# A clamped sum in one VectorE instruction, squares taken from it, and engines chosen pair by pair

## The chip, the cores and the metric

The kernel runs on 1 core of one Trainium2 chip. The metric is device microseconds for one execution; lower is better. Times of before are 736.77, 738.27 and 739.52 us, median 738.27 us.

The engines are called by the profile's names: PE is TensorE (matmuls), PEld its weight loads, DVE is VectorE, ACT is ScalarE, POOL is GpSimd, SP is SyncE, which here only issues DMAs. Each takes its instructions in program order.

## What is computed

Memory attention for 8 batches of 8 heads (576 tokens, head dimension 64, 32 memories), followed by a feed-forward block with a squared ReLU over the 4608 tokens:

```python
a = exp(phi - max(phi, axis=2)); a = a / (sum(a, axis=2) + 1e-9)
k_m, v_m = einsum('bhsm,bhsd->bhmd', a, k), einsum('bhsm,bhsd->bhmd', a, v)
scores = (1 / sqrt(64)) * q @ k_m.T
attn = exp(scores - max(scores)); attn = attn / (sum(attn) + 1e-9)
x = (attn @ v_m) as (4608, 512)
h = maximum(x @ w_in, 0)          # 512 -> 2048
out = (h * h) @ w_out             # 2048 -> 512
```

## The kernel before

Matmul operands in fp32r are carried as a high and a low part: ACT copies a value into `hi`, another engine writes `lo = value - hi`, and each product takes three matmuls. `w_in` is first multiplied into each batch's memories (`u`), so the first layer is `u` times the attention weights `a`.

Batches 0 to 2 (the first stage, to about 303 us) run one block of 128 hidden units and 288 tokens at a time. Batches 3 to 7 (the late stage) run in 40 pairs: a pair is two blocks of hidden units times two halves of 288 tokens, and its first layer is formed from 7 products of combined operands instead of 8 (`ffn1_product`, a scheme of Strassen's kind). The combined operands of the weights are made in `late_split`, those of the attention weights in `combine`. The 7 products land in three PSUM banks: two of `h`, which change places from pair to pair, and `z`. Four results of a pair come out of them:

- three by `from_sum`: ACT copies `z` into an SBUF tile `x` (`from_z`), DVE adds the `h` bank to it (line 1022), DVE clamps and squares in one instruction into `g` (line 1025), ACT copies `g` into `g_hi` (line 1026), POOL writes `g_lo` (line 1027), and for the second token half ACT also copies 64 columns aside (line 1029);
- one by `from_h`: ACT clamps the bank into `r` (line 1035), squares `r` into `g_hi` (line 1037), DVE multiplies `r` by `r` (line 1039) and subtracts (line 1040).

The second layer's 24 matmuls of a pair (line 984) are queued and issued between the first layer's products: `slot(k, n)` gives n of them in three parts, and ahead of each part `half(h)` issues whatever the plan has put at that half. A pair has 8 halves, a batch 64. The plan's lists (`late_plan`, `next_plan`, `first_plan`) hold, for each side task, the halves at which its steps are issued; numbers count from the batch's first half. Side tasks prepare the next batch: `late_exp` (softmax over phi, mostly DVE), `task_mem`, `late_attend`, `combine`, `late_u` (the products for `u` on PE into bank `m` and the free `h` bank, then two copies out, line 874), `late_split`, and loads on the SP queue (`late_stream` fetches the weights that `late_u` needs). The table `late_on` says for each named step whether POOL (1) or DVE (0) does it.

Of the kernel before, what the change touches and what calls it, by code (L numbers as in the profile page):

```python
# [7 lines left out]

# [16 lines left out]
def attn_moe_kernel(ctx: ExitStack, tc: tile.TileContext, qT, kv, phi, w_in, w_out, outT):  # L25
# [1330 lines left out]
    first_plan = [
        ((18,), task_q, 1, 0),
        ((-2,), task_kv, 1, 0),
        ((5, 9, 9, 10, 10, 13), task_exp, 1),
        ((16, 16, 16, 20), task_mem, 1),  # L1360
        ((26, 26, 27, 30, 30, 30, 31, 32), late_attend, 1, 0),
        ((37, 37, 39, 39, 40, 40, 42, 43), late_attend, 1, 1),
        ((0,), task_kv, 1, 1),
        ((44, 45, 45, 46, 47, 49), combine, 1),
        ((24,), late_stream, 1, 0),
        ((45, 46), late_u, 1, 0),
        ((33,), task_q, 1, 1),
        ((55,), late_stream, 1, 1),
        ((22, 23, 23, 24, 25, 26, 26, 27, 27, 28, 30, 30, 30), late_exp, 2),
        ((57, 57, 58, 59, 60), late_split, 1, 1),  # L1370
        ((21,), task_phi, 2),
        ((20,), task_kv, 2, 0),
# [231 lines left out]
```

## Time and profile before

| | before |
|---|---|
| median of three runs | 738.27 us |
| the profiled execution: time | 737.53 us |
| its span, first to last instruction | 735.7 us |
| busy in the span: PE, PEld | 704.5 us (96%), 588.6 us (80%) |
| DVE, ACT, POOL | 504.6 us (69%), 402.9 us (55%), 337.3 us (46%) |
| mean granted TensorE clock | 0.986 |

The profiled execution's time is 1.8 us more than its span: what lies ahead of the first instruction and behind the last. Its row counts a PE that has matmuls in flight as busy. The granted clock is a share of full speed, 2.4 GHz; half of that, 1.2 GHz, is its lower level.

### The profile page before, as it was taken

What the parts mean: (1) busy time and instruction counts of PE and PEld (TensorE: products, weight loads), DVE (VectorE), ACT (ScalarE), POOL (GpSimd) and SP (SyncE); (2) the same over time, 40 slices, a digit from 0 to 9 for tenths busy, and PEclk for the clock granted to TensorE, in tenths of its full rate; (3) what the DMA queues carried; (4) which work ended last, traced back from release to release, by engine and by line L of the source; (5) the groups of instructions that cost most, each with busy time, mean ns of one, the idle gap of its engine ahead of it and who ended that gap; (6) DMA issues with size and microseconds to landing.
All of it is one profiled execution on the core that took longest, in us unless ns stands there. A gap on an engine that the chain in (4) does not pass through costs nothing.

```text
span 735.7 us, 14219 instructions
## 1 busy us (share of the span) xinstructions
PE 704.5 (96%) x5242; PEld 588.6 (80%) x5242; DVE 504.6 (69%) x1070; ACT 402.9 (55%) x1042; POOL 337.3 (46%) x461
## 2 busy tenths in 40 slices
PE   7899999999999999999889998999899998999997
PEld 4367899899999899887668776787677877878897
DVE  4977757743545666578986788878887888565432
ACT  2657888865444256555445455655545555555431
POOL 1213255452432346465555455664655566555400
PEclk9999999999999999999999999999999999999999
DMA  9994453333076701282116511392112211310011
GB/s 309 346 352 189 141 154 127 109 99 147 33 179 194 201 33 58 98 246 90 58 57 190 156 58 58 114 253 93 58 48 102 90 57 58 115 58 1 0 58 37
DMA packets 65126, 88.81 MB, mean 121 GB/s; under 512 B 6432, under 2 KB 53856, under 8 KB 61600
## 3 DMA queue, kind: packets, MB, share of 16 engines
q1 hardware_dynamic: 63040, 86.33, 36.4%
q10 hardware_dynamic: 2016, 1.57, 0.7%
q8 instruction: 41, 0.67, 0.4%
q14 instruction: 29, 0.24, 0.1%
HBM read 74.25 MB, written 13.63 MB: 119 GB/s over the span
## 4 chain that ended last, share of the span: by engine, by line
PE 72%; DVE 17%; DMA 4%; ACT 4%; issue 2%; POOL 1%; SPq 0%; ACTq 0%; DVEq 0%; POOLq 0%
PE acc L984 20%; PE acc L669 16%; PE h L640 10%; PE h L1008 6%; PE z L1008 5%; PE acc L661 4%; DVE g_lo L1025 2%; PE h L1559 2%; PE ps_m L411 2%; PE m L411 2%; DMA wp<-in_w_in 2%; DMA e_sb<-in_phi 1%; DVE g_hi L1022 1%; DMA u_lo<-in_kv 1%; DVE low L906 1%
## 5 line engine op out<-in xcount | busy, mean ns | idle before, releaser
L984 PE MATMUL acc<-u_hi,wp 128*128 128x512 f32 x480 | 134.9, 401 | 0.0
L653 POOL TENSOR_TENSOR g_lo<-g,g_hi 128x288 fp32r<-128x288 f32 x80 | 71.2, 891 | 121.5 <-ACT g_hi L651 50.9
L984 PE MATMUL acc<-u_lo,wp 128*128 128x512 f32 x480 | 126.3, 400 | 0.0
L984 PEld LDWEIGHTS acc<-u_hi,wp 128*128 128x128 f32 x480 | 87.1, 189 | 34.8 <-issue 19.6
L895 POOL TENSOR_TENSOR u_lo<-low,u_hi 128x256 fp32r<-128x256 f32 (+1 forms) x133 | 89.9, 685 | 44.7 <-ACT u_hi L894 44.2
L984 PEld LDWEIGHTS acc<-u_lo,wp 128*128 128x128 f32 x480 | 90.8, 194 | 16.3
L669 PE MATMUL acc<-g_hi,wp 128*128 128x288 f32 x616 | 99.7, 298 | 0.0
L1027 POOL TENSOR_TENSOR u_hi<-g_lo,u_hi 128x288 fp32r<-128x288 f32 (+1 forms) x78 | 60.4, 775 | 72.8 <-ACT u_hi L1026 61.5
L669 PEld LDWEIGHTS acc<-g_hi,wp 128*128 128x128 f32 x616 | 87.7, 190 | 6.2 <-issue 2.8
L642 ACT ACTIVATE r<-h 128x288 f32<-128x288 f32 x96 | 39.3, 409 | 81.1 <-PE h L640 80.8
L894 ACT CAST u_hi<-low 128x256 fp32r<-128x256 f32 (+1 forms) x133 | 44.3, 351 | 42.5 <-DVE low L906 29.1
L669 PE MATMUL acc<-g_lo,wp 128*128 128x288 f32 x308 | 58.2, 297 | 0.0
L1026 ACT CAST u_hi<-g_lo 128x288 fp32r<-128x288 f32 (+1 forms) x78 | 31.6, 405 | 44.9 <-DVE g_lo L1025 43.8
L1022 DVE TENSOR_TENSOR g_hi<-h,g_hi 128x288 f32<-128x288 f32 x79 | 35.7, 451 | 18.4 <-ACT g_hi L1045 17.9
L669 PEld LDWEIGHTS acc<-g_lo,wp 128*128 128x128 f32 x308 | 47.1, 190 | 0.0
L1027 POOL TENSOR_TENSOR u_lo<-g_lo,u_lo 128x224 fp32r<-128x224 f32 x40 | 27.5, 688 | 41.8 <-ACT u_lo L1026 37.4
L1039 DVE TENSOR_TENSOR g_lo<-g 128x288 f32<-128x288 f32 x40 | 25.9, 648 | 28.4 <-ACT g L1035 28.3
L640 PE MATMUL h<-a_hi,u_hi 128*128 128x288 f32 x192 | 44.4, 317 | 0.6 <-DVE st L760 0.6
L1045 ACT COPY g_hi<-z 128x288 f32<-128x288 f32 x79 | 31.1, 393 | 25.5 <-PE z L1008 25.2
L648 DVE TENSOR_TENSOR g<-h,r 128x288 f32<-128x288 f32 x41 | 18.6, 453 | 35.5 <-ACT r L642 35.2
L1025 DVE SCALAR_TENSOR_TENSOR g_lo<-g_hi 128x288 f32<-128x288 f32 x78 | 41.0, 525 | 2.5
L640 PE MATMUL h<-a_hi,u_lo 128*128 128x288 f32 x176 | 37.5, 294 | 0.0
(335 smaller groups left out, 1677.6 us busy)
## 6 DMA issues: line engine op xcount, KB each, us to landing
w_sb<-w_f SPq DMA_DIRECT2D x23, 1024.0 KB, 4.9
wp<-in_w_in SPq DMA_DIRECT2D x16, 512.0 KB, 8.2
wp<-in_w_out SPq DMA_DIRECT2D x16, 512.0 KB, 6.8
q_sb<-in_q SPq DMA_DIRECT2D x28, 288.0 KB, 4.0
kvb<-in_kv SPq DMA_DIRECT2D x28, 256.0 KB, 5.8
tmp<-in_kv SPq DMA_DIRECT2D x24, 256.0 KB, 5.9
w_f<-w_sb SPq DMA_DIRECT2D x4, 1024.0 KB, 5.0
e_sb<-in_phi SPq DMA_DIRECT2D x7, 512.0 KB, 5.7
```

Of the source, the lines that this page charges most:

```text
L640: nc.tensor.matmul(h[:, :T], u[:, qd, fs], x[:, qd], start=(i == 0), stop=(i == len(todo) - 1))
L642: nc.scalar.activation(r, h[:, :T], AF.Relu)
L653: nc.gpsimd.tensor_tensor(out=g_lo, in0=g, in1=g_hi.bitcast(F32), op=ALU.subtract)
L669: nc.tensor.matmul(acc[e][:, :T], wo[f][:, w, e * P:(e + 1) * P], x, start=first and x is g_hi and w == 0, stop=last and x is g_lo,)
L894: nc.scalar.copy(hi[:, k], x)
L895: by(name).tensor_tensor(out=lo[:, k], in0=x, in1=hi[:, k].bitcast(F32), op=ALU.subtract)
L984: nc.tensor.matmul(late_accs[e], wo[f][:, w, e * P:(e + 1) * P], x, start=f == 0 and first, stop=f == NFT - 1 and last,)
L1008: nc.tensor.matmul(out[:, :T], u[:, lhs], a, start=first and not n, stop=n == 2, skip_group_check=not first)
L1022: nc.vector.tensor_tensor(out=x, in0=u[:, :T], in1=x, op=ALU.add)
L1025: nc.vector.scalar_tensor_tensor(out=g, in0=x, scalar=0.0, in1=x, op0=ALU.max, op1=ALU.mult)
L1026: nc.scalar.copy(g_hi, g[:, :n])
L1027: by(f"c{2 * fi + t}").tensor_tensor(out=g_lo, in0=g[:, :n], in1=g_hi.bitcast(F32), op=ALU.subtract)
```

## The change

`from_sum` forms the clamped sum with one custom DVE instruction (add, then clamp below at 0) into `x`; `g_hi` is then squared from `x` by ACT, and `g` is either a DVE product `x*x` or a second ACT square. `from_h` multiplies the PSUM bank by `r` instead of `r` by `r`, and its clamp may be done by DVE. The copy out of `z` may be done by DVE. `late_on` turns into a bit mask over the eight pairs of a batch, so that each of these choices, and those of `late_split` and `late_u`, differs by pair. Outside the pairs `sub1` and `at1` go to DVE, `mul1` and `b1` to POOL. The plan's halves are new, and `slot` gives 8, 11, 5 second-layer matmuls instead of 7, 11, 6.

```diff
     late_on = {
-        "top": 0, "sub0": 0, "sub1": 1, "sub2": 1, "at0": 0, "at1": 1, "mul0": 0, "mul1": 0,
-        "t3": 0, "t1": 0, "t2": 0, "t4": 0, "b0": 1, "b1": 0, "b2": 0, "b3": 1,
-        "b4": 0, "s1": 0, "s2": 0, "s3": 0, "s4": 0, "l0": 1, "l1": 1, "l2": 1,
-        "l3": 1, "c0": 1, "c1": 1, "c2": 0, "c3": 1, "raw0": 1, "raw1": 1,
+        "m0": 33, "m1": 253, "m3": 160, "fh": 5, "z1": 64, "z2": 4, "z3": 153, "top": 0,
+        "sub0": 0, "sub1": 0, "sub2": 1, "at0": 0, "at1": 0, "mul0": 0, "mul1": 1, "t3": 0,
+        "t1": 0, "t2": 0, "t4": 0, "b0": 1, "b1": 1, "b2": 0, "b3": 1, "b4": 0,
+        "s1": 53, "s2": 207, "s3": 58, "s4": 191, "l0": 187, "l1": 223, "l2": 223, "l3": 185,
+        "c0": 255, "c1": 253, "c2": 6, "c3": 239, "raw0": 14, "raw1": 15,
     }
-    def by(name):
-        return nc.gpsimd if late_on[name] else nc.vector
+    def by(name, p=0):
+        return nc.gpsimd if late_on[name] >> p & 1 else nc.vector
...
     def from_sum(j, fi, t, u, x, name="g_lo", bufs=3):
         g_hi, g_lo, n, kept = squared(j, fi, t)
-        nc.vector.tensor_tensor(out=x, in0=u[:, :T], in1=x, op=ALU.add)
+        nc.vector._custom_dve(TENSOR_ADD_SAT, out=x, in0=u[:, :T], in1=x, s0=float("inf"), s1=0.0)
         yield
         g = work.tile([P, T], F32, name=name, bufs=bufs)
-        nc.vector.scalar_tensor_tensor(out=g, in0=x, scalar=0.0, in1=x, op0=ALU.max, op1=ALU.mult)
-        nc.scalar.copy(g_hi, g[:, :n])
-        by(f"c{2 * fi + t}").tensor_tensor(out=g_lo, in0=g[:, :n], in1=g_hi.bitcast(F32), op=ALU.subtract)
+        nc.scalar.square(g_hi, x[:, :n])
+        if late_on[f"m{k}"] >> p & 1:
+            nc.scalar.square(g[:, :n], x[:, :n])
+        else:
+            nc.vector.tensor_tensor(out=g[:, :n], in0=x[:, :n], in1=x[:, :n], op=ALU.mult)
+        by(f"c{k}", p).tensor_tensor(out=g_lo, in0=g[:, :n], in1=g_hi.bitcast(F32), op=ALU.subtract)
         if kept is not None:
-            nc.scalar.copy(kept, g[:, n:])
+            nc.scalar.square(kept, x[:, n:])
     def from_h(j, fi, t, u):
-        nc.scalar.activation(r, u[:, :T], AF.Relu)
+        if late_on["fh"] >> p & 1:
+            nc.vector.tensor_scalar_max(r, u[:, :T], 0.0)
+        else:
+            nc.scalar.activation(r, u[:, :T], AF.Relu)
         yield
         nc.scalar.activation(g_hi, r[:, :n], AF.Square)
-        nc.vector.tensor_tensor(out=g[:, :n], in0=r[:, :n], in1=r[:, :n], op=ALU.mult)
-        by("c2").tensor_tensor(out=g_lo, in0=g[:, :n], in1=g_hi.bitcast(F32), op=ALU.subtract)
+        nc.vector.tensor_tensor(out=g[:, :n], in0=u[:, :n], in1=r[:, :n], op=ALU.mult)
+        by("c2", p).tensor_tensor(out=g_lo, in0=g[:, :n], in1=g_hi.bitcast(F32), op=ALU.subtract)
-    def from_z(name, bufs):
+    def from_z(j, k, name, bufs):
-        nc.scalar.copy(x, banks["z"][:, :T])
+        (nc.vector.tensor_copy if late_on[f"z{k}"] >> pairs[j][1] & 1 else nc.scalar.copy)(x, banks["z"][:, :T])
...
     late_plan = [
-        ((16, 16), late_u, 0, 2),
+        ((17, 17), late_u, 0, 2),
-        ((21,), late_stream, 0, 3),
+        ((31,), late_stream, 0, 3),
-        ((43, 43, 44, 45, 46), late_split, 0, 7),
+        ((39, 39, 41, 41, 43), late_split, 0, 7),
         ((0, 0), late_u, 0, 1),
         ((32, 32), late_u, 0, 3),
...
     next_plan = [
-        ((49, 49), late_u, 1, 0),
+        ((48, 49), late_u, 1, 0),
-        ((48, 49, 50, 51, 53, 54), combine, 1),
+        ((48, 50, 50, 51, 52, 56), combine, 1),
-        ((40, 40, 41, 41, 43, 44, 45, 46), late_attend, 1, 1),
+        ((40, 41, 41, 41, 44, 45, 46, 48), late_attend, 1, 1),
-        ((25, 25, 26, 26, 26, 29, 32, 32), late_attend, 1, 0),
+        ((25, 25, 25, 26, 26, 27, 32, 34), late_attend, 1, 0),
-        ((49, 49, 50, 55, 55), late_split, 1, 0),
+        ((51, 51, 51, 54, 55), late_split, 1, 0),
-        ((57, 57, 60, 62, 62), late_split, 1, 1),
+        ((57, 59, 59, 63, 63), late_split, 1, 1),
-        ((55, 56, 57, 58, 60, 60, 61, 63, 63, 63, 65, 66, 67), late_exp, 2),
+        ((59, 61, 61, 62, 65, 65, 65, 65, 67, 67, 67, 71, 71), late_exp, 2),
-        ((31,), task_q, 1, 1),
+        ((30,), task_q, 1, 1),
...
     first_plan = [
-        ((26, 26, 27, 30, 30, 30, 31, 32), late_attend, 1, 0),
+        ((29, 29, 29, 33, 33, 33, 35, 35), late_attend, 1, 0),
...
-        counts = {-1: (0, 9, 9), 0: (9, 9, 4)}.get(j, (7, 11, 6))
+        counts = {-1: (0, 9, 9), 0: (9, 9, 4)}.get(j, (8, 11, 5))
```

Lines of the plans are put in pairs here; their order in the file is another. The other entries of the plans move by a few halves as well.

## Rows read from the trace of the kernel before

**Rows 1.** The chain of work that ended last: share of the span by engine.

```profile
PE 72%; DVE 17%; DMA 4%; ACT 4%; issue 2%; POOL 1%; SPq 0%; ACTq 0%; DVEq 0%; POOLq 0%
```

**Rows 2.** Ten stretches, 228 to 728 us: busy us by engine, clock, DMA; their sum.

```profile
228.00:270.00 42.00, 39.68 (x374) 36.27 (x373) 25.54 (x66) 16.93 (x38) 14.22 (x22) 0.96 0.44 127
...
352.00:392.00 40.00, 34.64 (x192) 26.58 (x191) 34.44 (x72) 21.20 (x64) 24.38 (x30) 0.96 0.15 55
...
sum 500.00, PE 481.83 PEld 401.13 DVE 358.11 ACT 257.16 POOL 257.59; mean PE 48.18 PEld 40.11 DVE 35.81 ACT 25.72 POOL 25.76
```

**Rows 3.** The same view, first and last of five stretches with a lower clock.

```profile
248.00:256.00 8.00, 6.33 (x43) 5.18 (x43) 5.65 (x15) 1.57 (x4) 2.85 (x3) 0.79 0.50 133
...
610.00:618.00 8.00, 5.67 (x23) 4.81 (x22) 7.13 (x15) 3.99 (x12) 4.05 (x4) 0.79 0.38 131
```

**Rows 4.** What PE waited for longest: us in total, times, longest.

```profile
PE h L1008 <- ACT low L874: 11.6, 7, 2.3
```

**Rows 5.** Instructions in order of time, 359 to 364.5 us: start, duration, instruction.

```profile
359.40 0.61 PE L411 MATMUL h<-w_sb,mem 64*32 64x512 f32 x1
...
361.93 1.14 DVE L1025 SCALAR_TENSOR_TENSOR g_lo<-g_hi 128x288 f32<-128x288 f32 x1
...
363.54 0.58 ACT L874 COPY low<-h 128x512 f32<-128x512 f32 x1
...
364.17 0.40 PE L1008 MATMUL h<-u_hi,u_hi 128*128 128x288 f32 x1 [2.33 <-ACT low L874]
```

**Rows 6.** DVE groups, 352 to 388 us: count, busy us, mean ns, idle before.

```profile
L1025 DVE SCALAR_TENSOR_TENSOR g_lo<-g_hi 128x288 f32<-128x288 f32 x6 | 3.4, 566 | 0.2
...
L1039 DVE TENSOR_TENSOR g_lo<-g 128x288 f32<-128x288 f32 x3 | 2.3, 779 | 0.0
...
L906 DVE TENSOR_TENSOR low<-low,g_hi 128x128 f32<-128x128 f32 x3 | 1.8, 591 | 0.0
L736 DVE TENSOR_TENSOR e_sb<-e_sb,phi_mx 128x512 f32<-128x512 f32 x1 | 1.8, 1766 | 0.0
...
L724 DVE TENSOR_TENSOR top<-top 32x8 f32<-32x8 f32 x3 | 1.5, 494 | 0.1
L1025 DVE SCALAR_TENSOR_TENSOR g_lo<-g 128x288 f32<-128x288 f32 x3 | 1.4, 451 | 0.1
```

**Rows 7.** Two lines' durations in ns: min/median/max, first and last start.

```profile
L1022 DVE TENSOR_TENSOR g_hi<-h,g_hi x79: 440/451/459, 303.2 to 692.6; 128x288 f32<-128x288 f32 x79
...
L1039 DVE TENSOR_TENSOR g_lo<-g x40: 451/674/1076, 309.8 to 697.5; 128x288 f32<-128x288 f32 x40
```

**Rows 8.** Groups of the whole span, shapes kept apart.

```profile
L984 PE MATMUL acc<-u_hi,wp 128*128 128x512 f32 x480 | 134.9, 401 | 0.0
...
L895 POOL TENSOR_TENSOR u_lo<-low,u_hi 128x128 fp32r<-128x128 f32 x66 | 37.2, 574 | 15.0 <-ACT u_hi L894 14.9
...
L1037 ACT ACTIVATE u_lo<-g 128x288 fp32r<-128x288 f32 x40 | 17.9, 446 | 0.4
...
L562 DVE CUSTOM_DVE_ANT_0 w_sb<-tmp,low 128x2048 uint16<-128x2048 uint16 x4 | 5.3, 1322 | 0.3
```

**Rows 9.** Order of time about the first half of a batch: ACT, PE, DVE.

```profile
380.23 0.41 ACT L1035 ACTIVATE g<-h 128x288 f32<-128x288 f32 x1
...
380.99 0.61 PE L411 MATMUL h<-w_sb,mem 64*32 64x512 f32 x1
...
382.93 0.73 DVE L1039 TENSOR_TENSOR g_lo<-g 128x288 f32<-128x288 f32 x1
```

**Rows 10.** An issue on the SP queue; half 32 on PE and DVE; time to landing.

```profile
331.68 1.85 SPq L400 DMA_DIRECT2D q_sb<-in_q  x2
...
339.55 0.61 PE L411 MATMUL h<-w_sb,mem 64*32 64x512 f32 x1
...
339.95 0.71 DVE L1039 TENSOR_TENSOR g_lo<-g 128x288 f32<-128x288 f32 x1
...
w_sb<-w_f SPq DMA_DIRECT2D x4, 1024.0 KB, 4.9
```

More of the change, by code (lines that the diff above doesn't have):

```diff
@@ L7 @@
 from concourse._compat import with_exitstack
+from concourse.dve_ops import TENSOR_ADD_SAT
 F32 = mybir.dt.float32
@@ L894, in put @@
             nc.scalar.copy(hi[:, k], x)
-            by(name).tensor_tensor(out=lo[:, k], in0=x, in1=hi[:, k].bitcast(F32), op=ALU.subtract)
+            by(name, p).tensor_tensor(out=lo[:, k], in0=x, in1=hi[:, k].bitcast(F32), op=ALU.subtract)
         if b == JOIN and p < 3:
@@ L899, in late_split @@
         s = one.tile([P, 2, P], F32, name="phi_mx") if b == JOIN and p < 3 else work.tile([P, 2, P], F32, name="g_hi", bufs=3)
-        by("s1").tensor_tensor(out=s[:, 0], in0=raw[:, 3], in1=raw[:, 1], op=ALU.add)
-        by("s2").tensor_tensor(out=s[:, 1], in0=s[:, 0], in1=raw[:, 2], op=ALU.subtract)
+        by("s1", p).tensor_tensor(out=s[:, 0], in0=raw[:, 3], in1=raw[:, 1], op=ALU.add)
+        by("s2", p).tensor_tensor(out=s[:, 1], in0=s[:, 0], in1=raw[:, 2], op=ALU.subtract)
         yield
@@ L905, in late_split @@
         put(slice(2, 4), s, "l1")
-        by("s4").tensor_tensor(out=raw[:, 0], in0=raw[:, 0], in1=s[:, 1], op=ALU.subtract)
+        by("s4", p).tensor_tensor(out=raw[:, 0], in0=raw[:, 0], in1=s[:, 1], op=ALU.subtract)
         if b == JOIN and p < 3:
@@ L910, in late_split @@
         put(4, raw[:, 0], "l2")
-        by("s3").tensor_tensor(out=raw[:, 3], in0=raw[:, 2], in1=raw[:, 3], op=ALU.subtract)
+        by("s3", p).tensor_tensor(out=raw[:, 3], in0=raw[:, 2], in1=raw[:, 3], op=ALU.subtract)
         yield
@@ L1326, in attn_moe_kernel @@
     late_plan = [
-        ((10, 10, 10, 13, 14), late_split, 0, 3),
-        ((32, 32), late_u, 0, 3),
-        ((6, 6, 8, 8, 9), late_split, 0, 2),
-        ((0, 0), late_u, 0, 1),
-        ((16, 16), late_u, 0, 2),
-        ((4,), late_stream, 0, 2),
-        ((43, 43, 44, 45, 46), late_split, 0, 7),
-        ((21,), late_stream, 0, 3),
-        ((17, 17, 19, 19, 19), late_split, 0, 4),
-        ((27, 27, 28, 30, 30), late_split, 0, 5),
-        ((34, 35, 35, 35, 36), late_split, 0, 6),
+        ((6, 6, 7, 8, 10), late_split, 0, 2),
@@ L1338, in attn_moe_kernel @@
+        ((17, 17), late_u, 0, 2),
+        ((18, 18, 19, 20, 20), late_split, 0, 4),
+        ((26, 26, 27, 27, 30), late_split, 0, 5),
+        ((10, 10, 10, 11, 13), late_split, 0, 3),
+        ((39, 39, 41, 41, 43), late_split, 0, 7),
+        ((31,), late_stream, 0, 3),
+        ((1,), late_stream, 0, 2),
+        ((0, 0), late_u, 0, 1),
+        ((32, 32), late_u, 0, 3),
+        ((34, 34, 35, 37, 38), late_split, 0, 6),
     ]
     next_plan = [
-        ((36,), late_stream, 1, 0),
-        ((49, 49), late_u, 1, 0),
@@ L1355, in attn_moe_kernel @@
+        ((30,), task_q, 1, 1),
+        ((25, 25, 25, 26, 26, 27, 32, 34), late_attend, 1, 0),
+        ((60,), late_stream, 1, 1),
+        ((23,), task_phi, 2),
+        ((8, 8, 11, 16, 19, 20), task_mem, 1),
+        ((48, 49), late_u, 1, 0),
     ]
     first_plan = [
[L1357 to L1360, printed above, removed]
-        ((26, 26, 27, 30, 30, 30, 31, 32), late_attend, 1, 0),
-        ((37, 37, 39, 39, 40, 40, 42, 43), late_attend, 1, 1),
@@ L1363, in attn_moe_kernel @@
[L1363 to L1372, printed above, removed]
-        ((-5,), task_phi, 1),
-        ((28,), task_kv, 2, 1),
-        ((49, 49, 50, 51, 54), late_split, 1, 0),
+        ((8,), task_q, 1, 0),
@@ new lines, in attn_moe_kernel @@
+        ((43, 44, 44, 47, 47, 47), combine, 1),
+        ((29,), task_kv, 2, 0),
+        ((52, 52, 52, 54, 57), late_split, 1, 0),
+        ((37, 37, 38, 39, 41, 41, 41, 43), late_attend, 1, 1),
+        ((26,), late_stream, 1, 0),
+        ((29, 29, 29, 33, 33, 33, 35, 35), late_attend, 1, 0),
+        ((30,), task_q, 1, 1),
+        ((46,), late_stream, 1, 1),
+        ((22,), task_phi, 2),
+        ((37, 38), late_u, 1, 0),
+        ((-6,), task_phi, 1),
+        ((-13,), task_kv, 1, 1),
+        ((-11,), task_kv, 1, 0),
@@ L1376, in attn_moe_kernel @@
+        ((16, 17, 17, 18), task_mem, 1),
+        ((56, 56, 58, 59, 60), late_split, 1, 1),
+        ((29,), task_kv, 2, 1),
+        ((22, 23, 23, 24, 25, 25, 26, 27, 27, 28, 30, 30, 30), late_exp, 2),
+        ((3, 5, 5, 8, 10, 10), task_exp, 1),
     ]
@@ L1515, in attn_moe_kernel @@
             ffn1_product(z, j + 1, 2, True)
-            x = from_z("g_hi", 3) if old else from_z("r", 2)
+            x = from_z(j + 1, 2, *(("g_hi", 3) if old else ("r", 2)))
         if old:
```

19 lines of the change are left out of this document (10 added, 9 removed).

## The prediction

> **What bounds the kernel now.** I read the chain of waits first: 72% of the span runs through PE, and 17% through DVE, an engine that is busy for only 69% [rows 1]. So DVE is the bound in some stretch. The view by stretches shows where. From 228 to 728 us PE has matmuls in flight for 481.83 of 500 us. The 18.17 us that it lacks lie in five places: 5.36 us are gone between 352 and 392 us, 2.32 us between 228 and 270 us [rows 2], and the other three are the same stretch of the next three batches. In 352 to 392 us DVE is busy for 34.44 of 40 us, POOL for 24.38, ACT for 21.20 [rows 2]. Each of the five places is followed by 8 us in which the granted clock is 0.79, that is, at the lower level for 42% of the time [rows 3]. Half rate for 3.36 us loses 1.68 us; five times, 8.4 us.
>
> So there are 18.2 + 8.4 = 26.6 us to win at most, as long as PE's own work stays. The rest of the late stage is PE from end to end, and no other engine's work there is worth anything.
>
> What PE waits for is the next view: its largest wait is `h` (line 1008) for the ACT copies of line 874, 11.6 us in 7 waits [rows 4]. In order of time one of them reads so: `late_u` writes its results into the `h` bank at 359.40, the bank could be copied out from 360, but ACT takes its instructions in order and stands before a copy of `g` that DVE is late with. DVE starts that `g` at 361.93 and takes 1.14 us; the copy out runs at 363.54, and PE starts at 364.17 after 2.33 us without work [rows 5]. DVE's queue is late, ACT stands behind it, PE stands behind ACT.
>
> **What the change does to that stretch.** The 36 us from 352 to 388 hold three pairs (5 to 7) with one `late_split` each. In DVE time:
>
> - Nine clamp-and-squares of line 1025, six at 566 ns and three at 451 [rows 6], make 4.8 us. Of the nine squares that come in their place the masks leave three on DVE (`m0` of pairs 6 and 7, `m3` of pair 6): 3 x 0.57 = 1.7 us. Less 3.1 us.
> - The three products of line 1039 read two SBUF tiles and take 779 ns each here [rows 6]; over the span 451 to 1076 ns. The addition of line 1022 reads one bank of PSUM, has the same size and takes 440 to 459 ns in all 79 places [rows 7]. The new product reads the bank too: 0.45 us. Less 1.0 us.
> - Of the twelve small operations of `late_split`, four remain on DVE (`s1` and `s3` of pair 7, `s3` of pair 0, `s1` of pair 1). The dearest group, line 906, takes 591 ns [rows 6], the lighter ones less; at about 0.45 us the eight that go are 3.6 us.
> - `b1` goes, a subtract of 288 columns from SBUF, at line 1039's price 0.8 us [rows 6]; `at1` and `mul1`, two operations of one shape, change places: 0.
> - What comes: three copies out of `z` at the 0.45 us of line 1022, one copy of a double bank at ACT's 0.58 us [rows 5], `l3` of pair 1 at about 0.6: 2.5 us.
>
> The custom sum has no row. Below it is bounded by the addition that it replaces, 451 ns [rows 7], above by addition and clamp-and-square one after the other, 451 + 566 ns. The only custom instruction in the trace takes 1322 ns for 1024 words a partition [rows 8], which is 0.37 us for 288 words, so nothing there speaks for a slow one. I take 0.45 us, no change; the upper bound would add 9 x 0.57 = 5.1 us and undo nearly all of the rest.
>
> The sum is -3.1 - 1.0 - 3.6 - 0.8 + 2.5 = -6.0 us. Besides, `late_exp` starts 4 halves later, so that its six small steps (three of them at 494 ns), its subtract of 1.77 us [rows 6] and the two steps between them, some 5 us by estimate, fall into the next batch's first pair. DVE then has 34.4 - 6.0 = 28.4 us, or 23 without the moved part, in a stretch that takes 40 - 5.4 - 1.7 = 33 us when PE doesn't stop: 70 to 86% instead of a queue that is never empty. ACT gains six squares at 446 ns [rows 8] and loses four copies, +1 us. POOL gains eight small operations at 574 ns [rows 8] and `b1`, about +5 us, and passes `l3`: 24.4 + 4.6 = 29 of 33 us, 26 with its part of `late_exp` moved.
>
> The chain of a result gets shorter too: ACT's `g_hi` waits for the sum and no longer for sum and square, one operation of 0.45 to 1.14 us less ahead of the copies of line 874. And `late_u` of pair 6 is issued one half earlier than its copies out, so that eight instead of five second-layer matmuls cover them.
>
> I take three quarters of what the four late stretches lose: idle 18.17 - 2.32 = 15.85 us, clock 6.72 us; 0.75 x 22.6 = 16.9 us. Not all, since the order of each queue is fixed and short waits remain. In the first stage `late_attend` goes three halves behind a burst of `late_exp`; half of 2.32 + 1.68 us, 2.0 us. Together 18.9 us.
>
> **What it costs.** Two new waits on PE's own path.
>
> The `h` bank. Before, ACT's clamp of line 1035 was the last reader of the bank; now the DVE product is. The next user is a side task at the first half of the next pair (halves 0, 32, 40, and now 48). In the trace the clamp starts at 380.23 and ends at 380.64, the side task's matmuls write the bank at 380.99, and the product of line 1039 ran only from 382.93 to 383.66 [rows 9]. With a free DVE the product would end about 0.55 us behind the clamp, against 0.35 us here, and `slot` now gives one matmul less in between (134.9 us for 480, 0.28 us [rows 8]). A wait of some 0.4 us at 16 places (four in each of four batches): 7 us. The ends are 0 (the queue's other work lets PE run late anyway) and the 2.7 us of this place; at half 32 the product would have ended at 340.66, 1.1 us behind the side task's 339.55 [rows 10]. All that is queued on PE waits behind it. I take the low value, because what stood ahead of the product moves: the sum of `late_attend` from half 29 to 27, the small steps of `late_exp` from 60 to 65, `mul1` to POOL.
>
> The weights of `late_u`. `late_stream` for half 32 moves from half 21 to 31 and thereby behind `task_q`, which SP could issue only at 331.68 with 1.85 us for it, since it waits for `late_attend`'s matmuls at half 25; the weights land 4.9 us after their issue, near 338.5, and PE wants them at 339.55 [rows 10]. A margin of 1 us; I put 0.3 us at each of four places, 1.2 us. What stands behind it on SP has time.
>
> The sum against the profiled execution: 737.53 - 18.9 + 7.0 + 1.2 = 726.8 us. The median of the runs lies 0.74 us above that execution, so I predict 727.5 us.
>
> **A rule against it.** POOL's 574 ns for 128 columns [rows 8] stand against DVE's 591 ns for the same shape in the crowded stretch [rows 6]: nothing is lost by the move itself. The Trainium skill, "GPSIMD Engine Reference", 4.1 Engine selection, speaks against it: elementwise work of two inputs belongs on VectorE, GpSimd being about half as fast. By that rule the eight moves would cost POOL about 7 us where DVE saves 3.6, POOL would be at 32 of 33 us, and the sum would come out as rival (a) instead; no row here shows the factor of two.
>
> **The rivals.** Their times are on the scale of the median, 0.7 us above the profiled execution.
>
> (a) POOL takes DVE's place: 29 of 33 us is 88%, in order, behind ACT's copies, and DVE's transposes of `late_attend` now wait for POOL's `mul1`. Against it: the low parts are made about 8 halves, some 10 us, ahead of their use. If POOL is late the stretch stays as long as it is, and only the first stage's 2 us come back: 736 us. The Trainium skill, same page, 1 Specifications, says that GpSimd shares its SBUF interfaces with VectorE, so that each would slow the other; the spread of line 1039 against line 1022 [rows 7] agrees, and what more POOL work does to it no run here shows.
>
> (b) DVE stays the bound, because the custom sum or the squares cost more than I took. With the upper bound of 5.1 us DVE is back at 33 of 33 us, unless the moved `late_exp` gives room; if a quarter comes back instead of three, and the bank's waits fall half into stalls that are there anyway: 738.3 - 5.6 - 2.0 + 3.5 = 734 us.
>
> (c) The other side: the product holds the `h` bank at the 16 places as long as the old queue would have held it. The two places shown would have been late by 1.1 and 2.7 us [rows 9, 10], 1.9 us on average, 30 us in all: 738.3 - 18.9 + 30 + 1.2 = 751 us. It decides from 18.9 - 1.2 = 17.7 us, 1.1 us a place. For it speaks that all four places lie behind a pair's last operations; against it what is moved out of the way there.
>
> (d) The weights come 2 us late at each of four places: 727.5 - 1.2 + 8 = 734 us, and with a fall of the clock behind each (6.7 us) 741 us.
>
> **How the numbers follow.** Forecast 0.61: between 715 us (all of the 22.6 us and the first stage's 2.0, with the waits that I took: 738.3 - 24.6 + 1.2, no bank wait) and 733 us (half of the 22.6 us). (a) 0.11, (b) 0.11, (c) 0.12, (d) 0.05. Measurement tells about 0.5%, 3.7 us, from no change. Faster, below 734.6 us, takes the forecast, half of (b) and of (d) and a little of (a): 0.71. Slower, above 742 us: (c) and a part of (d), 0.14. Same: the rest, 0.15. The range leaves out most of (c) above and a twentieth below: 716 to 743 us.
>
> **What would show it.** Right: no wait of more than 1 us of `h` for line 874; no clock below 0.95 in the four stretches; DVE's share of the chain well under 17%; custom sums of 0.45 us; products of `from_h` at 0.45 us. Wrong: PE waiting for the line of that product at halves 0, 32, 40 and 48 by more than 0.6 us; custom sums of 0.8 us and more; POOL over 90% busy in the stretch with PE behind a low part; PE waiting for `w_sb`.

## The result, and the profile after

| | before | after |
|---|---|---|
| median, same chip (4 runs each) | 737.68 us | 709.11 us (707.37 to 710.30) |
| ratio | | 0.9608 (95%: 0.9579 to 0.9637) |
| profiled execution: time, span | 737.53, 735.7 us | 709.62, 707.8 us |
| mean granted clock | 0.986 | 0.998 |

The change makes the kernel 28.6 us faster. The forecast, 727.5 us with a range from 716 to 743, had the direction right and was 18.4 us too high; the time lies below its range.

The page of after, busy time by engine and the chain that ended last:

```profile
PE 691.2 (98%) x5242; PEld 583.3 (82%) x5242; DVE 466.5 (66%) x994; ACT 406.2 (57%) x1052; POOL 360.7 (51%) x527
...
PE 91%; DMA 7%; DVE 1%; SPq 1%; ACTq 0%; issue 0%; ACT 0%
```

DVE has gone from 17% of the chain [rows 1] to 1%, and PE now sets the time.

The windows of after: the stretches that answer to [rows 2] (the late one starts 6 us earlier here), the sum of ten, the same stretch without PE's stall of before, and the first place of the lower clock in [rows 3]:

```profile
226.00:268.00 42.00, 41.37 (x406) 37.38 (x404) 26.97 (x66) 17.63 (x39) 13.71 (x21) 1.00 0.48 130
...
346.00:386.00 40.00, 40.00 (x316) 32.49 (x315) 34.37 (x76) 25.00 (x75) 30.35 (x41) 1.00 0.25 84
...
sum 474.00, PE 471.51 PEld 398.77 DVE 321.42 ACT 261.42 POOL 281.51; mean PE 47.15 PEld 39.88 DVE 32.14 ACT 26.14 POOL 28.15
...
346.00:379.00 33.00, 33.00 (x211) 26.63 (x210) 28.19 (x61) 19.74 (x61) 25.92 (x35) 1.00 0.19 63
...
248.00:256.00 8.00, 7.37 (x64) 6.35 (x63) 6.65 (x17) 1.94 (x5) 3.34 (x9) 1.00 0.81 167
```

PE has matmuls in flight for all of 40 us where it lacked 5.36, lacks 2.5 us in 474 where it lacked 18.17 in 500, and the clock stays at its upper level. DVE is hardly less busy in those 40 us, 34.37 against 34.44 or 86% both times, while more of the kernel is done in them: it stays as full as it was, and PE no longer stops.

PE's waits in the late stage are down to one row; the 11.6 us of [rows 4] are gone. All of the chain's links named in [rows 5, 9, 10] show in the order of time of after: `late_u` of pair 6, the first half of a batch, and the weights at half 32.

```profile
356.01 0.61 PE L412 MATMUL h<-w_sb,mem 64*32 64x512 f32 x1
...
356.87 0.46 DVE L1026 CUSTOM_DVE_ANT_0 g_hi<-h,g_hi 128x288 f32<-128x288 f32 x1
...
357.36 0.39 ACT L1029 ACTIVATE u_hi<-g_hi 128x224 fp32r<-128x224 f32 x1 [1.70 <-DVE g_hi L1026]
...
358.09 0.57 ACT L876 COPY low<-h 128x512 f32<-128x512 f32 x1
...
358.96 0.29 PE L1010 MATMUL h<-u_hi,u_hi 128*128 128x288 f32 x1
...
372.13 0.39 ACT L1046 ACTIVATE g<-h 128x288 f32<-128x288 f32 x1
...
372.63 0.45 DVE L1050 TENSOR_TENSOR g_lo<-h,g 128x288 f32<-128x288 f32 x1
...
373.83 0.61 PE L412 MATMUL h<-w_sb,mem 64*32 64x512 f32 x1
...
404.91 0.89 SPq L401 DMA_DIRECT2D q_sb<-in_q  x2
...
405.85 9.79 SPq L858 DMA_DIRECT2D w_sb<-w_f  x2
...
414.12 0.61 PE L412 MATMUL m<-w_sb,mem 64*32 64x512 f32 x1 [1.27 <-DMA w_sb<-w_f]
```

The copy out of `h` (line 876, 874 before) starts 2.08 us after the first write into the bank, against 4.14 us in [rows 5], and PE's next product has no wait. At the batch's first half the product reads the bank from 372.63 to 373.08 and the side task comes at 373.83: 0.75 us to spare. At half 32 PE does wait for the weights, 1.27 us.

The two durations that answer to [rows 7], the custom sum and the product from the bank (min/median/max in ns):

```profile
L1026 DVE CUSTOM_DVE_ANT_0 g_hi<-h,g_hi x79: 440/457/460, 301.1 to 664.5; 128x288 f32<-128x288 f32 x79
...
L1050 DVE TENSOR_TENSOR g_lo<-h,g x40: 393/450/459, 307.3 to 669.8; 128x288 f32<-128x288 f32 x40
```

Where the time went is best seen pair by pair: from the first `z` matmul of a pair to that of the next, read from the order of time. All 40 pairs took 389.3 us from the first to the last start before and 363.4 after. One batch, the third of the late stage, in us, with the kernels of the experiments beside it:

| pair | 0 | 1 | 2 | 3 | 4 | 5 | 6 | 7 | batch |
|---|---|---|---|---|---|---|---|---|---|
| before | 10.83 | 10.87 | 9.53 | 9.15 | 9.89 | 9.66 | 13.41 | 8.35 | 81.7 |
| after | 9.53 | 10.83 | 9.52 | 9.15 | 10.19 | 9.15 | 9.52 | 8.29 | 76.2 |
| `e2_plan_alone` | 11.44 | 12.70 | 10.91 | 9.75 | 9.62 | 9.81 | 11.37 | 8.45 | 84.1 |
| `e4_engines_alone` | 11.21 | 11.92 | 9.53 | 11.22 | 9.63 | 10.39 | 11.51 | 12.00 | 87.4 |
| `e1_old_plan` | 11.05 | 11.86 | 9.72 | 9.77 | 9.63 | 9.90 | 12.05 | 9.61 | 83.6 |
| `e8_forms_and_plan` | 11.41 | 11.06 | 9.56 | 9.25 | 10.31 | 9.49 | 9.85 | 8.39 | 79.3 |
| `f1_chain_back` | 11.05 | 12.70 | 10.63 | 9.72 | 10.12 | 9.50 | 11.37 | 8.41 | 83.5 |
| `e6_early_load` | 9.53 | 11.07 | 9.52 | 9.15 | 9.53 | 9.15 | 9.53 | 8.29 | 75.8 |

Over the four batches pair 6 gives back 15.1 us and the pair 0 behind it 7.4 us.

### The profile page after: what moved, and what is told of

The parts are those of the page before. It is cut to its first block, busy times and chain, and to the rows that moved or that the text cites. A ratio compares the mean times of both kernels' runs of the same rounds, so it can differ in the third digit from the quotient of the medians.

```text
span 707.8 us, 14201 instructions
## 1 busy us (share of the span) xinstructions
PE 691.2 (98%) x5242; PEld 583.3 (82%) x5242; DVE 466.5 (66%) x994; ACT 406.2 (57%) x1052; POOL 360.7 (51%) x527
## 4 chain that ended last, share of the span: by engine, by line
PE 91%; DMA 7%; DVE 1%; SPq 1%; ACTq 0%; issue 0%; ACT 0%
PE acc L986 31%; PE acc L670 18%; PE h L641 11%; PE h L1010 9%; PE z L1010 6%; PE acc L662 4%; PE m L412 3%; DMA w_sb<-w_f 2%; PE h L1570 2%; PE ps_m L412 2%; DMA wp<-in_w_in 2%; DMA u_lo<-in_kv 1%; DMA e_sb<-in_phi 1%; PE m L1570 1%; PE z L1570 1%; PE h L325 1%
## 5 line engine op out<-in xcount | busy, mean ns | idle before, releaser
L986 PE MATMUL acc<-u_hi,wp 128*128 128x512 f32 x480 | 128.1, 399 | 0.0
L986 PE MATMUL acc<-u_lo,wp 128*128 128x512 f32 x480 | 123.1, 392 | 0.0
L986 PEld LDWEIGHTS acc<-u_lo,wp 128*128 128x128 f32 x480 | 88.0, 188 | 15.4
L1034 POOL TENSOR_TENSOR u_hi<-g_lo,u_hi 128x224 fp32r<-128x224 f32 (+1 forms) x73 | 56.4, 773 | 44.9 <-ACT g_lo L1031 44.6
L897 POOL TENSOR_TENSOR u_lo<-low,u_hi 128x128 fp32r<-128x128 f32 (+1 forms) x98 | 62.5, 643 | 17.1 <-ACT u_hi L896 16.4
L1026 DVE CUSTOM_DVE_ANT_0 g_hi<-h,g_hi 128x288 f32<-128x288 f32 x79 | 35.9, 454 | 22.0 <-ACT g_hi L1056 20.7
L1029 ACT ACTIVATE u_hi<-g_hi 128x224 fp32r<-128x224 f32 x79 | 32.5, 412 | 18.1 <-DVE g_hi L1026 18.1
L1056 ACT COPY g_hi<-z 128x288 f32<-128x288 f32 x69 | 27.4, 397 | 24.4 <-PE z L1010 24.2
L649 DVE TENSOR_TENSOR g<-h,r 128x288 f32<-128x288 f32 x41 | 18.5, 452 | 32.0 <-ACT r L643 31.8
L641 PE MATMUL h<-a_lo,u_hi 128*128 128x288 f32 x176 | 37.5, 294 | 0.0
L652 ACT ACTIVATE g_hi<-r 128x288 fp32r<-128x288 f32 x80 | 35.0, 437 | 3.0
```

Of the source, the lines that this page charges most:

```text
L641: nc.tensor.matmul(h[:, :T], u[:, qd, fs], x[:, qd], start=(i == 0), stop=(i == len(todo) - 1))
L652: nc.scalar.activation(g_hi, r, AF.Square)
L897: by(name, p).tensor_tensor(out=lo[:, k], in0=x, in1=hi[:, k].bitcast(F32), op=ALU.subtract)
L986: nc.tensor.matmul(late_accs[e], wo[f][:, w, e * P:(e + 1) * P], x, start=f == 0 and first, stop=f == NFT - 1 and last,)
L1026: nc.vector._custom_dve(TENSOR_ADD_SAT, out=x, in0=u[:, :T], in1=x, s0=float("inf"), s1=0.0)
L1034: by(f"c{k}", p).tensor_tensor(out=g_lo, in0=g[:, :n], in1=g_hi.bitcast(F32), op=ALU.subtract)
```

## The experiments

Four theories stood against each other: that DVE's work fell (the prediction's); that the new halves of the plan alone moved work out of the crowded stretch; that engine table and plan fit only each other; and that ACT's place in its queue is what counts, since ACT no longer stands behind DVE's second operation. Each kernel is told as an edit of after, unless it says otherwise; ratios are to before on the same chip.

**The change in three parts.** The parts are the forms (`from_sum`, `from_h`), the engine table (with the masks for `z`, and, where the new forms are there, for the squares and the clamp) and the plan (with the `slot` counts). Every combination was timed.

`e1_old_plan`: forms and engines, all halves of the plan and the counts as before.

```diff
-        ((48, 49), late_u, 1, 0),
+        ((49, 49), late_u, 1, 0),
...
-        counts = {-1: (0, 9, 9), 0: (9, 9, 4)}.get(j, (8, 11, 5))
+        counts = {-1: (0, 9, 9), 0: (9, 9, 4)}.get(j, (7, 11, 6))
```

> The changed kernel with the old plan (the halves of all side tasks, and 7, 11, 6 matmuls a slot): only forms and engines are new. If the work taken off VectorE decides (theory 1), the crowded stretch has room wherever its steps are issued, and the time is within 6 us of the changed kernel: 709 to 715 us. If the new halves decide (theory 2), it keeps most of the old stalls: 728 to 737 us. If each gives about half: 718 to 726 us.

`e2_plan_alone`: the kernel before with the new plan and counts.

```diff
-        counts = {-1: (0, 9, 9), 0: (9, 9, 4)}.get(j, (7, 11, 6))
+        counts = {-1: (0, 9, 9), 0: (9, 9, 4)}.get(j, (8, 11, 5))
```

> The kernel before with the new plan and the new 8, 11, 5 matmuls a slot; forms and engines are the old ones. Theory 1 (the work on VectorE decides): 731 to 739 us. Theory 2 (the halves decide): 711 to 718 us. About half each: 720 to 728 us. In the old forms the bank of h is freed by ScalarE's clamp, so no wait for the product can show here.

`e3_forms_alone`: the kernel before with the new forms, all squares of the sums on DVE.

```diff
-        nc.vector.tensor_tensor(out=x, in0=u[:, :T], in1=x, op=ALU.add)
+        nc.vector._custom_dve(TENSOR_ADD_SAT, out=x, in0=u[:, :T], in1=x, s0=float("inf"), s1=0.0)
...
-        nc.scalar.copy(g_hi, g[:, :n])
+        nc.scalar.square(g_hi, x[:, :n])
```

> The kernel before with the new forms of from_sum and from_h alone (custom sum, squares on VectorE, product from the bank); old plan, old engines. If the shorter chain to g_hi is worth something by itself (theory 3), the 2.3 us stalls shrink: 728 to 735 us. If the product of from_h now holds the h bank behind an old, full VectorE queue (the prediction's rival c; in the run with the old plan TensorE starts 0.05 to 0.09 us behind the product's end at halves 0, 32 and 49), it is slower: 740 to 748 us.

`e4_engines_alone`: the kernel before with the new table. `e7_old_forms`: the same and the new plan. Both are after with this undone (and, in `e4_engines_alone`, the plan):

```diff
-        nc.scalar.square(g_hi, x[:, :n])
+        nc.vector.scalar_tensor_tensor(out=g, in0=x, scalar=0.0, in1=x, op0=ALU.max, op1=ALU.mult)
+        nc.scalar.copy(g_hi, g[:, :n])
...
-        nc.vector.tensor_tensor(out=g[:, :n], in0=u[:, :n], in1=r[:, :n], op=ALU.mult)
+        nc.vector.tensor_tensor(out=g[:, :n], in0=r[:, :n], in1=r[:, :n], op=ALU.mult)
```

> The kernel before with the new table of engines alone, pair by pair; old forms (sum, clamp-and-square, copies) and old plan. If the work taken off VectorE counts wherever it stands (theory 1): 725 to 734 us. If steps moved to GpSimd and copies moved to VectorE come late in the old order and TensorE waits for them instead (theory 4: table and plan fit each other and nothing else): 735 to 743 us.

> The changed kernel with the old forms of from_sum and from_h; new engines and new plan stay. VectorE then squares in all 24 places of a batch instead of 13, and ScalarE's copies wait for the squares. If the forms carry the gain together with the plan: 725 to 738 us. If engines and plan carry it: 709 to 716 us.

`e8_forms_and_plan`: after with the old engine table.

```diff
-        "m0": 33, "m1": 253, "m3": 160, "fh": 5, "z1": 64, "z2": 4, "z3": 153, ...
+        "m0": 0, "m1": 0, "m3": 0, "fh": 0, "z1": 0, "z2": 0, "z3": 0, ...
```

> The changed kernel with the old engines: all squares on VectorE, all of late_split's sums on VectorE, copies out of z on ScalarE; new forms and new plan stay. If the table of engines carries the gain together with the plan: 725 to 740 us. If forms and plan carry it: 709 to 716 us.

| forms | engines | plan | kernel | median us | ratio (95%) |
|---|---|---|---|---|---|
| new | old | old | `e3_forms_alone` | 732.27 | 0.9939 (0.9913 to 0.9964) |
| old | new | old | `e4_engines_alone` | 762.92 | 1.0346 (1.0312 to 1.0380) |
| old | old | new | `e2_plan_alone` | 740.60 | 1.0045 (1.0022 to 1.0068) |
| new | new | old | `e1_old_plan` | 742.39 | 1.0079 (1.0051 to 1.0107) |
| old | new | new | `e7_old_forms` | 731.22 | 0.9917 (0.9886 to 0.9947) |
| new | old | new | `e8_forms_and_plan` | 718.40 | 0.9749 (0.9718 to 0.9779) |
| new | new | new | after | 709.11 | 0.9608 (0.9579 to 0.9637) |

The parts don't add up: alone they come to -0.6 + 3.5 + 0.5 = +3.3%, together to -3.9%. The theory that the halves alone do it falls with `e2_plan_alone`. The one that table and plan fit only each other holds in part: on the old plan the table costs 3.5% with the old forms (its largest PE wait in the late stage, from its list of waits below, is for `z`, which the new table lets DVE copy out) and 1.4 points with the new forms, and on the new plan it gains 1.3 to 1.4 points with either. The forms are worth 3 points on the new plan with either table, 2.7 on the old plan with the new table, and only 0.6 with plan and table old.

Four of these expectations were missed: `e1_old_plan`, `e2_plan_alone` and `e4_engines_alone` came out slower than every range put down for them, and `e8_forms_and_plan` between its two.

```profile
PE z L1010 <- DVE g L1049: 14.9, 8, 2.5
```

**What the forms do.** ACT's waits are a view that the prediction made no use of. Of before, from 300 to 700 us (us in total, times, longest):

```profile
ACT u_hi L1026 <- DVE g_lo L1025: 43.8, 32, 2.2
ACT u_lo L1026 <- DVE g_lo L1025: 39.9, 31, 2.9
```

For 83.7 us ACT stood before a copy of `g` until DVE's clamp-and-square came. The late copy out of [rows 5] is one of these places; ACT's order of time in before:

```profile
363.11 0.38 ACT L1026 CAST u_hi<-g_lo 128x224 fp32r<-128x224 f32 x1 [2.13 <-DVE g_lo L1025]
363.39 0.24 ACT L1029 COPY o<-g_lo 128x64 f32<-128x64 f32 x1
363.54 0.58 ACT L874 COPY low<-h 128x512 f32<-128x512 f32 x1
```

The same list of after, and of `e8_forms_and_plan`, in which all squares `g` are still DVE's:

```profile
ACT u_hi L896 <- POOL low L908: 28.8, 29, 2.0
...
ACT u_hi L1029 <- DVE g_hi L1026: 18.1, 25, 2.0
```

```profile
ACT u_hi L1025 <- DVE g_hi L1022: 13.1, 21, 1.0
```

What is left of that wait is for the sum: 22.3 us in after and 18.5 in `e8_forms_and_plan`, with the rows for `u_lo` (4.2 and 5.4 us). `f1_chain_back` takes `e8_forms_and_plan` and gives ACT's wait back, with the custom sum, DVE's squares and all engines kept; DVE only squares 64 columns more in two squares of three.

```diff
-        nc.scalar.square(g_hi, x[:, :n])
...
-            nc.vector.tensor_tensor(out=g[:, :n], in0=x[:, :n], in1=x[:, :n], op=ALU.mult)
+            nc.vector.tensor_tensor(out=g, in0=x, in1=x, op=ALU.mult)
+        nc.scalar.copy(g_hi, g[:, :n])
...
-            nc.scalar.square(kept, x[:, n:])
+            nc.scalar.copy(kept, g[:, n:])
```

> The kernel with new forms, new plan and old engines (718 us) with one thing undone: ScalarE makes g_hi and the 64 kept columns as a copy of g, behind VectorE's square, and not as its own square of the clamped sum. VectorE has exactly the same work. If ScalarE standing in its queue behind VectorE's second operation is the cause (theory 5: 84 us of such waits in the kernel before, 28 us in the 718 us kernel), most of the 22 us that the forms gave on this plan go: 732 to 742 us. If the cause is VectorE's work (theory 1), it stays at 717 to 721 us.

It took 738.10 us, 1.0002 (0.9981 to 1.0024): all of the gain of forms and plan, 2.5%, is gone. Its ACT waits are back at 51.9 + 51.3 us, and the order of time shows the link:

```profile
ACT u_hi L1029 <- DVE g_lo L1028: 51.9, 37, 2.7
ACT u_lo L1029 <- DVE g_lo L1028: 51.3, 40, 2.4
```

```profile
479.51 0.45 DVE L1028 TENSOR_TENSOR g_lo<-g_hi 128x288 f32<-128x288 f32 x1
...
480.00 0.38 ACT L1029 CAST u_hi<-g_lo 128x224 fp32r<-128x224 f32 x1 [2.71 <-DVE g_lo L1028]
```

The edit also makes each result's own chain longer, since `g_hi` now follows `g`, and that could be the cause instead of ACT's queue. PE's waits in the late stage tell the two apart. Of `f1_chain_back`, and of `e8_forms_and_plan`:

```profile
PE z L1006 <- ACT g L1052: 8.4, 17, 0.9
PE h L1006 <- ACT low L872: 2.4, 7, 0.5
```

```profile
PE z L1006 <- ACT g L1052: 0.7, 4, 0.2
```

In `f1_chain_back` PE waits for ACT's other copies, out of `z`, out of `h` and for two more (14.4 us in all, against 0.7), and no row has it waiting for a `u_hi` or a low part: what is late is what stands behind the copy of `g` in ACT's queue.

DVE's work does not decide between these two. The batch of the table above, from its pair 0 to the next batch's, in the windows of before, `e8_forms_and_plan`, `f1_chain_back` and after, one each (the third busy time is DVE's):

```profile
464.80:546.50 81.70, 78.64 (x538) 62.11 (x537) 67.61 (x160) 44.58 (x136) 47.67 (x70) 0.98 0.38 117
```

```profile
451.00:530.30 79.30, 77.47 (x538) 61.08 (x537) 66.96 (x160) 45.46 (x136) 48.20 (x70) 1.00 0.40 120
```

```profile
463.30:546.80 83.50, 79.10 (x538) 60.76 (x538) 65.47 (x159) 44.77 (x136) 47.18 (x71) 1.00 0.36 114
```

```profile
450.10:526.30 76.20, 75.61 (x538) 61.16 (x537) 59.87 (x145) 45.13 (x136) 53.00 (x83) 1.00 0.42 125
```

`e8_forms_and_plan` has 160 DVE instructions and 67 us of DVE work a batch, as before, and is 2.5% faster; `f1_chain_back` has 1.5 us less and gains nothing. Only the last step, from `e8_forms_and_plan` to after, goes with less DVE work, 59.9 us.

On the old plan the same forms do much less. `e3_forms_alone` has no ACT wait for DVE's square either, and pair 6 takes 10.1 to 10.3 us in its four batches where before took 12.3 to 13.7. But pair 4 is longer (10.4 to 10.5 us against 9.6 to 10.0), pair 0 takes 11.9 us in three batches (10.8 to 13.5 before), and PE waits for the bank that the product now holds (4.0 us) and for `z` (4.6 us); 0.6% is left.

`g4_chain_back_in_full` makes the same edit in after itself, where the masks let ACT make some of the squares `g` too.

```diff
-        nc.scalar.square(g_hi, x[:, :n])
...
+        nc.scalar.copy(g_hi, g[:, :n])
...
-            nc.scalar.square(kept, x[:, n:])
+            nc.scalar.copy(kept, g[:, n:])
```

> The changed kernel, all new, but ScalarE again makes g_hi and the kept columns as a copy of g and not as a square of the clamped sum. VectorE does the same work but for 64 more columns in some squares; ScalarE waits for VectorE's square where that is on VectorE (13 of 24 places). Theory 5 (ScalarE behind VectorE in its queue is the cause): 720 to 732 us. If the shorter chain matters only where VectorE is full: 709 to 714 us.

719.55 us, 0.9755 (0.9718 to 0.9791): 10.4 us lost, not 20, and just under the 720 to 732 us expected. Where ACT squares for itself there is no DVE to stand behind, so here ACT's largest wait for DVE's square is this one (with 9.1 us more for `u_hi`):

```profile
ACT u_lo L1033 <- DVE g_lo L1032: 29.9, 21, 1.8
```

So on the new plan the order of the chain and the engine table stand in for each other: without the one 10.4 us are lost, without the other 9.3 us, without both 29 us (by the ratios 1.5, 1.4 and 3.9 points; the medians are of different chips).

**The engine table by its parts.** Three kernels put one group of masks back each: the copies out of `z` to ACT, the small steps of `late_split` to the old engines, the squares `g` to DVE.

```diff
-        "z1": 64, "z2": 4, "z3": 153,
+        "z1": 0, "z2": 0, "z3": 0,
```

> The changed kernel with all copies out of z on ScalarE again; all else new. ScalarE gets 6 copies of 0.4 us a batch, VectorE loses them. If these copies come late behind VectorE (with the table on the old forms TensorE waited 14.9 us for them), ScalarE does them better now that it waits little: 705 to 709 us. If ScalarE gets too full: 711 to 718 us.

```diff
-        "s1": 53, "s2": 207, "s3": 58, "s4": 191, "l0": 187, "l1": 223, "l2": 223, "l3": 185,
+        "s1": 0, "s2": 0, "s3": 0, "s4": 0, "l0": 255, "l1": 255, "l2": 255, "l3": 255,
```

> The changed kernel with late_split's engines as before (its sums on VectorE, its low parts on GpSimd). Of the 10 us that the table of engines gives on top of forms and plan, this tells the part of late_split: if the small sums on VectorE are what fills the crowded stretch, 715 to 720 us; if not, 709 to 712 us.

```diff
-        "m0": 33, "m1": 253, "m3": 160,
+        "m0": 0, "m1": 0, "m3": 0,
```

> The changed kernel with all 24 second squares of a batch on VectorE (13 in the changed kernel), 11 more of 0.45 to 0.6 us. If VectorE's work is what the table of engines eases: 713 to 720 us. If the order of the queues is enough: 709 to 712 us.

They took 713.86 (0.9684, 0.9661 to 0.9708), 714.84 (0.9698, 0.9672 to 0.9724) and 714.46 us (0.9691, 0.9661 to 0.9722): each group is worth some 5 us, none the whole. `g3_squares_on_dve` came out in the range that stood for DVE's work: for this last step the load does count. `g2_small_steps_back` lies just under its upper range (715 to 720). Each loses in pairs of its own: `z` on ACT in pair 2 (9.52 to 10.1 us in all four batches), the small steps in pair 6 (9.52 to 10.3) and in three batches pair 7 (8.3 to 9.1), the squares in pair 7 of three batches (8.3 to 9.0 or more).

**Single steps of the plan.** `f2_late_exp_back` puts `late_exp` two to five halves earlier again, near its old place; `f3_late_u_back` issues `late_u` of pair 6 at its old half.

```diff
-        ((59, 61, 61, 62, 65, 65, 65, 65, 67, 67, 67, 71, 71), late_exp, 2),
+        ((57, 58, 58, 59, 60, 60, 61, 63, 63, 63, 65, 66, 67), late_exp, 2),
```

> The changed kernel with late_exp two to eight halves earlier, nearly at its old halves (57 to 67, old 55 to 67, new 59 to 71). If room in the crowded stretch comes from this move, the first pairs of a batch get longer again: 714 to 725 us. If the shorter chain leaves enough room: 709 to 711 us.

```diff
-        ((48, 49), late_u, 1, 0),
+        ((49, 49), late_u, 1, 0),
```

> The changed kernel with late_u of pair 6 issued at half 49 again, its copies out with it, five second-layer matmuls ahead of the next use of the bank and not eight. If these matmuls cover the copies: about 1 us a batch in four batches, 712 to 715 us. If ScalarE is on time anyway: 709 to 710 us.

`late_exp` is worth 11 us: 720.25 us, 0.9746 (0.9704 to 0.9787). Pair 7 goes from 8.3 to 10.5 us in three batches, and PE waits for `z` again, which DVE copies out:

```profile
PE z L1010 <- DVE g L1056: 6.1, 3, 2.1
```

The earlier `late_u` is worth nothing that can be measured: 710.48 us, 0.9625 (0.9590 to 0.9659).

**The two costed waits.** `e5_r_times_r` lets `from_h` multiply `r` by `r` again, so that the bank is free after the clamp; `f4_old_plan_r_times_r` does so in `e1_old_plan`; `e6_early_load` puts the load of the weights back to half 21.

```diff
-        nc.vector.tensor_tensor(out=g[:, :n], in0=u[:, :n], in1=r[:, :n], op=ALU.mult)
+        nc.vector.tensor_tensor(out=g[:, :n], in0=r[:, :n], in1=r[:, :n], op=ALU.mult)
```

> The changed kernel, but the product of from_h takes r times r from SBUF again, so that ScalarE's clamp frees the h bank and not VectorE's product. If holding the bank costs TensorE time, as the prediction had it (0.4 us at 16 places, 7 us), this runs at about 702 us. If the bank is free in time anyway, as the order of instructions in the changed kernel reads (0.16 to 1.8 us to spare at all 30 places), it stays at 709 us, or comes out 0 to 3 us slower, since the product from two SBUF tiles takes up to twice as long.

> New forms and engines on the old plan (742 us) with the product of from_h taken from r times r, so that ScalarE's clamp frees the h bank. There TensorE started 0.05 to 0.09 us behind the end of that product at halves 0, 32 and 49. If the held bank is a loss of its own in the old plan (rival c of the prediction): 730 to 738 us. If the stall only moves on to the next thing that is late: 740 to 744 us.

```diff
-        ((31,), late_stream, 0, 3),
+        ((21,), late_stream, 0, 3),
```

> The changed kernel with one load moved back: the weights for half 32 are fetched at half 21 and not at 31, ahead of the q load on the SP queue. The two pairs that took 10.84 and 10.19 us instead of 9.53 should lose their wait of 1.9 us for the weights: 707.2 us. Rival: the 1 MB then meets the loads of kv and phi, these come late in their place, and nothing is won or 1 to 3 us are lost.

The bank costs nothing in after: `e5_r_times_r` takes 709.53 us, 0.9637 (0.9603 to 0.9670). On the old plan the wait is real. `e1_old_plan` at the first half of the second late batch:

```profile
376.56 0.41 ACT L1046 ACTIVATE g<-h 128x288 f32<-128x288 f32 x1
...
380.63 0.45 DVE L1050 TENSOR_TENSOR g_lo<-h,g 128x288 f32<-128x288 f32 x1
...
381.13 0.61 PE L412 MATMUL h<-w_sb,mem 64*32 64x512 f32 x1 [0.47 <-DVE g_lo L1050]
```

The clamp is done at 376.97, the product only at 381.08, and PE starts behind it. Without it, `f4_old_plan_r_times_r` takes 739.29 us, 1.0023 (1.0001 to 1.0044), 0.6 points less and between its two expected ranges. Pair 0 loses its 1.3 us of excess, but pair 6 then takes 11.1 to 13.7 us: part of the stall moves on.

The weights: `e6_early_load` takes 706.64 us, 0.9596 (0.9568 to 0.9624), the lowest time measured here. Its interval overlaps that of after, but the row of PE waiting for `w_sb` (1.9 us) is gone, and pair 4 takes 9.51 to 9.53 us in all batches, where after has 10.84 and 10.19 in two.

## Why the prediction was too high, point by point

**Read rightly.** The place (four stretches of the late stage, where pair 6 and the pair 0 behind it gave back 22.5 of the 25.9 us, and one in the first stage; the 36 us from 352 to 388 are not quite pairs 5 to 7, which run from 348.6 to 380.4 us, but reach into the next batch's pair 0); the mechanism's shape, DVE late, ACT behind it, PE behind ACT; the unit costs, custom sum 457 ns and bank product 450 ns against 450 and 450; POOL not the bound, 25.92 us of 33 against 26 to 29; DVE at 28.19 us of 33 against 23 to 28.4. The Trainium skill's rule that was weighed ("GPSIMD Engine Reference", 4.1) would have given rival (a); line 908 of after, the same shape as line 906 on DVE in [rows 6], took 583 ns on POOL against 591. But those 591 ns are DVE's price in its crowded stretch. Line 911 of before, of that shape too, has a median of 280 ns on DVE over the span, half of POOL's 574 in [rows 8], and line 913 of after, 20 times on each engine, 282 ns on DVE and 461 on POOL. So the trace of before did show the factor, and after a factor of 1.6; rival (a) did not come all the same, since PE waits for no low part in after's late stage.

The first stage gave 2.1 us (302.2 to 300.1 at the late stage's start) against 2.0, but this agreement is not shown: `e5_r_times_r`, `e6_early_load`, `f2_late_exp_back` and `f3_late_u_back`, whose first stage is that of after, reach the late stage at 299.55, 299.43, 301.82 and 297.60 us.

**The step that failed: "three quarters of what the four late stretches lose", 16.9 us.** The late stage gave back 25.9 us, and 27.9 us with the 2.0 us that it now pays for the weights. That is more than all of the 22.6 us that were said to be there at most. Two things were wrong in it.

First, the share. It came from DVE's load: I read the stall as a queue that is never empty, and took work off it. The runs show that for 20 of the 29 us the load is beside the point (`e8_forms_and_plan` against `f1_chain_back`: equal load, 20 us apart, on the new plan and the old table). What counted there is that ACT, in order, stood behind DVE's second operation (83.7 us in before, 103.2 in `f1_chain_back`) and held back all else in its queue. The prediction gave this one sentence ("the chain of a result gets shorter too") and no price. The last 9 us, the engine table's, go with less work on DVE.

Second, the cap. The 22.6 us are idle time and clock. PE's row counts matmuls in flight as busy, so a wait that is bridged in part by matmuls in flight doesn't show in full. Pairs 4 and 5 of the four batches show it, here by the windows of before (sum over the four; the clock is 1.00 in each):

```profile
sum 77.40, PE 76.10 PEld 58.84 DVE 65.19 ACT 41.74 POOL 47.56; mean PE 19.03 PEld 14.71 DVE 16.30 ACT 10.43 POOL 11.89
```

PE lacked 1.3 us of 77.4, yet the same eight pairs, with as many matmuls, take 74.6 us in `e6_early_load`: 1.5 us were lost while PE counted as busy. That the rest of the 5.3 us above the cap is of this kind is an inference and not shown.

**The `h` bank, 7 us, measured 0.** The forecast took the 0.35 us between clamp and side task from [rows 9] as fixed. It was a symptom itself: the clamp was late because ACT was. In before it starts 1.1 to 2.0 us behind the matmuls that fill its bank at 15 of the 16 places, in after 0.1 to 0.5 us at all of them. So in after it ends 1.3 to 1.4 us ahead of the side task at halves 0, 40 and 48, 1.0 to 2.4 us at half 32, and the product fits in between, with 0.16 to 1.77 us to spare at all 30 side tasks. The old plan shows that the mechanism exists (rival (c), by `e1_old_plan`), at 0.6 points there.

**The weights, 1.2 us, measured 2.0**: 1.3 and 0.7 us at two places instead of 0.3 at four. PE waiting for `w_sb` was among the prediction's signs of being wrong; it came, and costs 2 us without undoing the gain.

The sum, on the profiled execution: 726.8 - 11.0 (late stretches, 27.9 against 16.9) - 7.0 (bank) + 0.8 (weights) - 0.1 (first stage) = 709.5 us; measured 709.62. The rest of the 18.4 us lies between the profiled executions and the medians, 0.74 us at before and 0.5 us at after.

**Open.** The 25 us that the engine table costs on the old plan are explained for 14.9 us (PE waiting for `z` behind a DVE copy); the rest wasn't separated. Why the forms need the new plan to be worth 3 points is told by the rows of `e3_forms_alone` only in part. Of the plan's halves only `late_exp`, `late_u` of pair 6 and the load of the weights were tried one by one.

## What to carry to other kernels

Where an engine takes its instructions in order, read whom it waits for, not only how busy it is: an instruction at the head of ACT's queue that needs DVE's second result charges DVE's lateness to everything behind it, and computing the same value from an earlier result (a square of the sum instead of a copy of the square) was worth 10 to 20 us at nearly equal DVE work, on the new plan; on the old one all the new forms together gave 4 us. A gap or a slack read in the slow kernel may be a product of the same stall; before it is used as a term, ask what it would be without it. And a change in engines and a change in order are to be tried together: here each cost time alone.

## What was not expected of the hardware

The small 32x8 operations of `late_exp`, 494 ns each in [rows 6] (line 724, 726 in after), took 155 ns in the same stretch of after, while the product of line 1033, which reads SBUF alone, still took 790 (the groups of DVE from 346 to 382 us):

```profile
L1033 DVE TENSOR_TENSOR g_lo<-g_hi 128x288 f32<-128x288 f32 x3 | 2.4, 790 | 0.0
...
L726 DVE TENSOR_TENSOR top<-top 32x8 f32<-32x8 f32 x3 | 0.5, 155 | 0.1
```

What stretched them before wasn't tested. And in after the pairs of the late stage, but for the very first, have fixed lengths, 8.3 us of matmuls alone, 9.5 with `late_u`, 9.15 with `late_attend`, 10.8 with `task_mem`, to within 0.1 us wherever PE doesn't wait; a pair's length is then itself the measure of a stall.
